# Key and value tiles as unbroken 512 KB runs of the cache

## The chip, the core and the metric

The kernel runs on one core of one Trainium2 chip. The metric is device time in microseconds, from a set of timed runs, and beside it stands the hardware profile of one execution. The core has a matrix engine (PE, with PEld for its weight loads), a vector engine (DVE), a scalar engine (ACT), a general engine (POOL) and a sequencer (SP, SyncE) from which this kernel issues nearly all its DMAs. Sixteen DMA engines carry the transfers from HBM into the on-chip buffer of 128 partitions.

## What is computed

Decoding of one token for four batch entries, through two layers that share all weights: attention against a cache of 4,096 positions, then a gated dense block, and both once more.

```
x: (4, 1, 512)   k_cache, v_cache: (4, 8, 4096, 128)   wq: (512, 4096)   wo: (4096, 512)
w_gate, w_up: (512, 1792)   w_down: (1792, 512)          all bf16

attention(x): q = x @ wq, 32 heads of 128, four query heads to one key head
              p = softmax(q . k / sqrt(128)) over the 4096 positions
              o = sum over positions of p * v;   return o @ wo
dense(x):     (gelu(x @ w_gate) * (x @ w_up)) @ w_down

x = x + attention(layernorm(x));  x = x + dense(layernorm(x))
x = x + attention(layernorm(x));  x = x + dense(layernorm(x))
```

The sum over positions and the softmax do not depend on the order of the positions, as long as a key and its value carry the same number.

## The kernel before

**Tiles.** For one batch entry and one key head, the keys are 4,096 rows of 256 B, 1 MB in one piece in HBM; the values likewise. Position number is 32 times the partition plus a column from 0 to 31: `(p c) d -> p c d`. A tile is one half of the columns (t = 0 or 1, 16 columns, `CH`), so 128 partitions x 4,096 B = 512 KB. In HBM a tile is every other 4 KB of the head's 1 MB.

**Keys.** `Keys` loads the sixteen key tiles of one batch entry, group of four heads by group, and in a group first all t = 0, then all t = 1. `load` (L405) takes one tile with one DMA (L409); `load_pairs` (L411) takes the same half of two neighbouring heads in one DMA of 1 MB (L416). Buffers are `KP`, two heads to a buffer; `KT` are views of one head in it. `turn` transposes a key tile in place on DVE (L424), and `scores` multiplies the turned tile with the queries on PE (L435). The keys of a batch entry stay in the buffer between layer 1 of this entry and its layer 2.

**Values.** `VRing` holds seven slots (`V_SLOTS`) of one tile each. Its list `seq` names the tiles in the order in which they will be needed, and `pump` (L527) issues a DMA (L533) for the next ones as soon as a slot is free. `Values.step` multiplies a tile's sixteen columns with the probabilities on PE (L576), gives the slot back and pumps again. `Streamed.fill` (L611) does it for the values of layer 2 that are taken up while the next dense layer runs (PE at L625). At the end, in `attend_last`, the key buffers are free, and `pump_head` (L536) loads both halves of a value head into one pair buffer with one DMA of 1 MB (L540); some single tiles go into key buffers too, by `pump`.

**Order.** The order of all work is written out by hand. Batch entries run one after another: dense layer of entry b, then `attend(b + 1)`, which does layer 2 of entry b and layer 1 of entry b + 1. The first entry has `attend_first`, the last `attend_last` and `dense_last`. All loads are issued from SP (`dq`) in program order, each behind the wait for its buffer; the weights of the output projection and the dense block (`load_rest`) are loaded once, after the first attention. The lines of the tile's source:

```
def cache_tile(cache, b, kvh, t):
    return cache[b, kvh].rearrange("(p c) d -> p c d", p=P)[:, t * CH:(t + 1) * CH]
...
dq.dma_start(out=KT[kvh][t], in_=cache_tile(A_k_cache, self.b, kvh, t))      # L409
dq.dma_start(out=v, in_=cache_tile(A_v_cache, *key[1:]))                      # L533
```

Of the kernel before, what the change touches and what calls it, by code (L numbers as in the profile page):

```python
# [15 lines left out]
P = 128  # L16
# [9 lines left out]
GH = 4  # L26
CH = 16
# [6 lines left out]
def kernel(  # L34
# [24 lines left out]
    NT = C // CH  # L59
# [25 lines left out]
    dq = nc.sync  # L85
# [6 lines left out]
    KP = [[[wts.tile([P, 2, CH, Dh], BF16, name=f"kp{g}_{t}_{j}") for j in range(GH // 2)]  # L92
           for t in range(NT)] for g in range(NG)]
# [35 lines left out]
        return v.unsqueeze(1).broadcast_to([P, WIDE // n, n])  # L129

    def cache_tile(cache, b, kvh, t):
        return cache[b, kvh].rearrange("(p c) d -> p c d", p=P)[:, t * CH:(t + 1) * CH]

    def load_wq(g):
        n = HG * Dh
# [258 lines left out]
    class Keys:  # L394
# [10 lines left out]
        def load(self, count):  # L405
            for _ in range(count):
                kvh, t = self.tile(self.nl)
                self.nl += 1
                dq.dma_start(out=KT[kvh][t], in_=cache_tile(A_k_cache, self.b, kvh, t))  # L409

        def load_pairs(self, count):  # L411
            for _ in range(count):
                kvh, t = self.tile(self.nl)
                self.nl += 2
                pair = A_k_cache[self.b, kvh:kvh + 2].rearrange("h (p c) d -> p h c d", p=P)
                dq.dma_start(out=KP[kvh // GH][t][kvh % GH // 2][:],  # L416
                             in_=pair[:, :, t * CH:(t + 1) * CH])

        def turn(self, count=1):
            for _ in range(count):  # L420
# [96 lines left out]
    class VRing:  # L517
# [9 lines left out]
        def pump(self, spare=None):  # L527
            free = self.free if spare is None else spare
            while self.at < len(self.seq) and free:
                key = self.seq[self.at]  # L530
                self.at += 1
                v = free.pop(0)
                dq.dma_start(out=v, in_=cache_tile(A_v_cache, *key[1:]))  # L533
                self.ready[key] = (v, spare is None)

        def pump_head(self, pair):  # L536
            (layer, b, kvh, t), other = self.seq[self.at:self.at + 2]
            assert t == 0 and other == (layer, b, kvh, 1)
            self.at += 2
            dq.dma_start(out=pair.rearrange("p t c d -> p (t c) d"),  # L540
                         in_=A_v_cache[b, kvh].rearrange("(p c) d -> p c d", p=P))
            for t in range(NT):
                self.ready[(layer, b, kvh, t)] = (pair[:, t], False)

# [498 lines left out]
```

## Time and profile before

| what | value |
|---|---|
| timed runs, median (lowest to highest of 3) | 306.95 us (304.64 to 307.58) |
| profiled execution, span from first to last instruction | 303.8 us (the page gives no other time of it) |
| mean granted TensorE clock | 0.788 |
| busy: PE, PEld, DVE, ACT, POOL | 193.5, 133.4, 157.0, 43.5, 0.7 us |
| read from HBM over the span | 106.17 MB, 350 GB/s |
| DMA from value cache to v_t | 103 of 512 KB, median 7.9 us from issue to landing |
| DMA from key cache to kp | 40 of 512 KB (13.2 us) and 12 of 1 MB (6.0 us) |
| DMA from value cache to kp | 3 of 1 MB (12.3 us) and 3 of 512 KB (12.0 us) |

An engine's busy time is the time in which it worked on an instruction; weight loads overlap matmuls, and several engines work side by side, so the times are not to be added. The DMA share is the mean busy share of the sixteen DMA engines, and a packet's time in it may overlap the next one's a little, so that a share of 1.02 to 1.03 is a full queue. The time from issue to landing holds the wait behind earlier loads in the queue. A wait names what released it last.

### The profile page before, as it was taken

The page shows a single profiled execution, that of the slowest core. Times are in us where ns is not written, and L with a number is a line of the kernel's source. Part 1 is how long each engine was busy: PE and PEld are TensorE (multiplying, and loading weights), DVE is VectorE, ACT ScalarE, POOL GpSimd, SP SyncE. Part 2 cuts the span into 40 slices and gives each one's busy share as a digit, 9 for nine tenths or more (in the row PEclk, how much of TensorE's full clock was granted, in tenths as well). Part 3 has the DMA queues.
Part 4 walks back from the last instruction along what each step waited for, and adds up shares of the span by engine and source line. Part 5 has one row for each costly group of instructions (what it writes and reads, how often), then busy time and mean ns, then how long its engine had stood idle before and what let it go on. Part 6 is the DMA issues. An engine that isn't in the chain of part 4 may idle for free.

```text
span 303.8 us, 10133 instructions
## 1 busy us (share of the span) xinstructions
PE 193.5 (64%) x4593; PEld 133.4 (44%) x4593; DVE 157.0 (52%) x399; ACT 43.5 (14%) x109; POOL 0.7 (0%) x6
## 2 busy tenths in 40 slices
PE   1466085342684837778838367799373678889884
PEld 0214044332642524556616144566161355565673
DVE  3584913002238896326568983155579931454323
ACT  2001002000012020213201202032121020132200
POOL 0000000000000000000000000000000000000000
PEclk9999997555558675969996859689958597589977
DMA  6999999999439999999999999999999999988900
GB/s 252 367 420 422 416 416 410 368 401 407 173 109 371 404 420 417 417 401 320 344 352 417 419 419 416 412 274 338 357 412 415 420 412 358 337 288 308 415 36 5
DMA packets 32898, 106.83 MB, mean 352 GB/s; under 512 B 2772, under 2 KB 8664, under 8 KB 32472
## 3 DMA queue, kind: packets, MB, share of 16 engines
q1 hardware_dynamic: 32840, 106.19, 90.3%
q8 instruction: 36, 0.59, 0.8%
q14 instruction: 6, 0.05, 0.1%
q10 hardware_dynamic: 16, 0.00, 0.0%
HBM read 106.17 MB, written 0.00 MB: 350 GB/s over the span
## 4 chain that ended last, share of the span: by engine, by line
DMA 61%; PE 25%; DVE 5%; SPq 5%; issue 2%; ACT 1%; DVEq 0%; ACTq 0%
DMA v_t<-in_A_v_cache_dram 34%; DMA kp<-in_A_k_cache_dram 21%; DMA wd_sb<-in_B_w_down_dram 5%; PE sc L435 5%; PE ot L576 4%; PE q L224 4%; PE so L625 3%; PE g L224 2%; SPq L141 2%; PE yr L286 2%; DVE qb L249 1%; PE y L224 1%; DVE pp L462 1%; SPq L142 1%; PE x L481 1%
## 5 line engine op out<-in xcount | busy, mean ns | idle before, releaser
L424 DVE STREAM_TRANSPOSE kp<-kp 128x1024 f32<-128x1024 f32 x64 | 75.4, 1216 | 7.3 <-DMA kp<-in_A_k_cache_dram 7.3
L576 PE MATMUL ot<-pe,v_t 128*128 128x32 bf16 x1520 | 50.2, 184 | 29.6 <-DMA v_t<-in_A_v_cache_dram 26.1
L576 PEld LDWEIGHTS <-v_t 128*128 128x128 bf16 x1520 | 45.3, 102 | 44.4 <-DMA v_t<-in_A_v_cache_dram 33.2
L435 PE MATMUL sc<-kp,qb 128*32 128x512 bf16 x512 | 46.9, 457 | 13.8 <-DVE kp L424 10.2
L435 PEld LDWEIGHTS <-qb 128*32 128x32 bf16 x512 | 14.6, 104 | 34.5 <-issue 18.3
L454 ACT ACTIVATE pp<-sc,nm 128x512 bf16<-128x512 f32 x16 | 11.0, 687 | 128.7 <-DVE junk L450 106.7
L515 DVE TENSOR_TENSOR OT_bf<-ot,rden 128x32 bf16<-128x32 f32 (+3 forms) x34 | 6.0, 176 | 43.9 <-PE ot L576 43.8
L224 PE MATMUL q<-xb,wq_sb 128*128 128x32 bf16 (+1 forms) x640 | 18.5, 176 | 7.0 <-DMA wq_sb<-in_A_wq_dram 7.0
L224 PEld LDWEIGHTS <-wq_sb 128*128 128x128 bf16 x640 | 17.3, 99 | 10.9 <-DMA wq_sb<-in_A_wq_dram 8.0
L441 DVE TENSOR_REDUCE m<-sc 128x1 f32<-128x512 f32 x16 | 10.9, 680 | 15.0 <-PE sc L435 14.9
L481 PE MATMUL x<-pp,ident_bf 128*32 128x128 bf16 x256 | 8.2, 260 | 15.4 <-DVE pp L462 15.4
L467 PE MATMUL den<-zx,mean_f 128*128 128x16 f32 x32 | 8.4, 340 | 13.2 <-DVE qb L249 13.2
L224 PE MATMUL y<-OT_bf,wo_sb 128*128 128x32 bf16 x256 | 8.8, 187 | 8.0 <-DMA wo_sb<-in_A_wo_dram 7.5
L467 PEld LDWEIGHTS den<-zx,mean_f 128*128 128x128 f32 x32 | 6.8, 265 | 15.7 <-issue 15.2
L481 PEld LDWEIGHTS <-ident_bf 128*32 128x32 bf16 x256 | 5.5, 109 | 18.0 <-issue 17.3
L625 PE MATMUL so<-v_t,pl 128*32 128x512 bf16 x96 | 11.5, 470 | 1.0 <-DMA v_t<-in_A_v_cache_dram 0.7
L224 PEld LDWEIGHTS <-wo_sb 128*128 128x128 bf16 x256 | 8.1, 103 | 8.8 <-DMA wo_sb<-in_A_wo_dram 8.0
L224 PE MATMUL g<-xb,wg_sb 128*128 128x32 bf16 x280 | 9.0, 187 | 4.2 <-DMA wg_sb<-in_B_w_gate_dram 3.1
L462 DVE STREAM_TRANSPOSE pp<-pp 128x512 bf16<-128x512 bf16 x16 | 11.1, 691 | 0.9 <-ACT pp L454 0.9
L304 DVE TENSOR_TENSOR xb<-XX,y 128x4 bf16<-128x4 f32 (+1 forms) x9 | 1.6, 173 | 18.2 <-PE y L224 18.2
L224 PEld LDWEIGHTS <-wg_sb 128*128 128x128 bf16 x280 | 8.1, 104 | 5.7 <-DMA wg_sb<-in_B_w_gate_dram 3.2
L224 PE MATMUL u<-xb,wu_sb 128*128 128x32 bf16 x280 | 8.6, 183 | 2.6 <-DMA wu_sb<-in_B_w_up_dram 2.6
(120 smaller groups left out, 169.3 us busy)
## 6 DMA issues: line engine op xcount, KB each, us to landing
v_t<-in_A_v_cache_dram SPq DMA_DIRECT2D x103, 512.0 KB, 7.9
kp<-in_A_k_cache_dram SPq DMA_DIRECT2D x40, 512.0 KB, 13.2
kp<-in_A_k_cache_dram SPq DMA_DIRECT2D x12, 1024.0 KB, 6.0
wq_sb<-in_A_wq_dram SPq DMA_DIRECT2D x2, 2048.0 KB, 11.5
wo_sb<-in_A_wo_dram SPq DMA_DIRECT2D x4, 1024.0 KB, 6.6
kp<-in_A_v_cache_dram SPq DMA_DIRECT2D x3, 1024.0 KB, 12.3
wg_sb<-in_B_w_gate_dram SPq DMA_DIRECT2D x1, 1792.0 KB
wu_sb<-in_B_w_up_dram SPq DMA_DIRECT2D x1, 1792.0 KB
```

The lines of the kernel that those rows point to most:

```text
L141: dq.dma_start(out=wo_sb[:, i * n:(i + 1) * n], in_=wo_dram[:, i * n:(i + 1) * n])
L224: nc.tensor.matmul(dst, lhsT=lhsT, rhs=rhs, start=first, stop=last, skip_group_check=True)
L286: nc.tensor.matmul(self.rows[j:j + B], lhsT=self.o[:, i], rhs=wo_sb[:, i], start=False, stop=True, skip_group_check=True)
L424: nc.vector.transpose(out=words, in_=words)
L435: nc.tensor.matmul(sc[s * QS:(s + 1) * QS], lhsT=qb[:, w0:w0 + 2 * W], rhs=kt[:, :, be // 2, :, be % 2], start=(t == 0 and be == 0), stop= ...
L441: nc.vector.tensor_reduce(out=m[:], in_=sc.rearrange("p c j -> p (c j)"), axis=AX.X, op=ALU.max)
L454: nc.scalar.activation(out=pp[:], in_=sc[:], func=ACT.Exp, bias=nm[:, 0:1], scale=scale, accum_out=ls[:])
L462: nc.vector.transpose(out=flat, in_=flat)
L467: nc.tensor.matmul(den[:], lhsT=mean_f[:, 0:1].broadcast_to([P, P]), rhs=zx[:], start=True, stop=True)
L481: nc.tensor.matmul(x[a * QS:(a + 1) * QS, s], lhsT=ident_bf[:, s * QS:(s + 1) * QS], rhs=pT[:, a], start=True, stop=True, skip_group_check ...
L576: nc.tensor.matmul(self.ot[:, s % 2], lhsT=v[:, i, :], rhs=wide(pe[:, s, t * CH + i, :]), start=(done == 0 and i == 0), stop=(done == NT - ...
L625: nc.tensor.matmul(ps[j * QS:(j + 1) * QS], lhsT=pe[:, s, w:w + 2 * QD].rearrange("p c h -> p (c h)"), rhs=v[:, j * QD:(j + 1) * QD].rearr ...
```

## The change

A position's number becomes 2,048 times t plus 16 times the partition plus a column from 0 to 15, for keys and values alike. Tile t is then the first or the second half of the head's positions, one piece of 512 KB in HBM, of which each partition takes the next 4 KB. Pairs of key heads take such a piece of each of the two heads. `pump_head` still loads the whole 1 MB of a head into the same buffer, but a partition's 8 KB now come from two places 512 KB apart.

```diff
     def cache_tile(cache, b, kvh, t):
-        return cache[b, kvh].rearrange("(p c) d -> p c d", p=P)[:, t * CH:(t + 1) * CH]
+        return cache[b, kvh].rearrange("(t p c) d -> t p c d", t=NT, p=P)[t]
...
-                pair = A_k_cache[self.b, kvh:kvh + 2].rearrange("h (p c) d -> p h c d", p=P)
-                dq.dma_start(out=KP[kvh // GH][t][kvh % GH // 2][:],
-                             in_=pair[:, :, t * CH:(t + 1) * CH])
+                pair = A_k_cache[self.b, kvh:kvh + 2].rearrange("h (t p c) d -> t p h c d",
+                                                                t=NT, p=P)
+                dq.dma_start(out=KP[kvh // GH][t][kvh % GH // 2][:], in_=pair[t])
...
-            dq.dma_start(out=pair.rearrange("p t c d -> p (t c) d"),
-                         in_=A_v_cache[b, kvh].rearrange("(p c) d -> p c d", p=P))
+            dq.dma_start(out=pair[:],
+                         in_=A_v_cache[b, kvh].rearrange("(t p c) d -> p t c d", t=NT, p=P))
```

## The prediction

> **What bounds the kernel now.** I read the DMA row of the page's slices first, then the DMA queues, the chain that ended last, the table by stretches, SP's waits and last the single packet records of the trace.
>
> The DMA rows of the slices (mean busy tenths of the 16 DMA engines, then GB/s, 7.6 us to a slice):
>
> ```profile
> DMA  6999999999439999999999999999999999988900
> GB/s 252 367 420 422 416 416 410 368 401 407 173 109 371 404 420 417 417 401 320 344 352 417 419 419 416 412 274 338 357 412 415 420 412 358 337 288 308 415 36 5
> ```
>
> The DMA engines work nearly all the time, but at two speeds: about 416 GB/s in long stretches, and 270 to 370 GB/s in others where the busy digit is still 9. The only long holes are slices 10 and 11 (nothing left to load before the first dense layer ends) and the last two (all data in).
>
> The queue that carries all loads, with its packets, MB and share of 16 engines over the span, and the heads of the chain:
>
> ```profile
> q1 hardware_dynamic: 32840, 106.19, 90.3%
> ...
> DMA 61%; PE 25%; DVE 5%; SPq 5%; issue 2%; ACT 1%; DVEq 0%; ACTq 0%
> ```
>
> 106.19 MB at 416 GB/s is 255 us of the 303.8 us span. DMA is 61% of the chain, and 34% plus 21% of the span in it are value and key tiles, the very loads that change.
>
> The table by stretches (start and end, length, busy time of PE, PEld, DVE, ACT, POOL, then TensorE's granted clock, DMA share and GB/s):
>
> ```profile
> 8.00:12.00 4.00, 2.14 (x68) 1.97 (x68) 0.81 (x5) 0.00 (x0) 0.00 (x0) 1.00 0.97 328
> 12.00:52.00 40.00, 19.80 (x337) 11.18 (x337) 24.50 (x38) 3.34 (x8) 0.00 (x0) 0.96 1.02 418
> 88.00:104.00 16.00, 11.47 (x277) 8.11 (x270) 12.00 (x25) 3.23 (x8) 0.00 (x0) 0.73 0.97 361
> 104.00:136.00 32.00, 20.68 (x457) 13.37 (x451) 18.45 (x37) 3.93 (x9) 0.00 (x0) 0.76 1.02 415
> 136.00:148.00 12.00, 10.72 (x275) 7.66 (x275) 7.03 (x28) 3.75 (x10) 0.00 (x0) 0.93 0.93 336
> 148.00:161.00 13.00, 6.93 (x173) 4.67 (x165) 8.54 (x20) 2.65 (x7) 0.00 (x0) 0.89 0.96 348
> 197.00:210.00 13.00, 11.79 (x296) 8.44 (x296) 7.56 (x31) 3.75 (x10) 0.00 (x0) 0.92 0.95 324
> 210.00:222.00 12.00, 5.91 (x146) 3.87 (x139) 7.01 (x18) 1.78 (x5) 0.00 (x0) 0.90 0.93 333
> 253.00:275.00 22.00, 18.61 (x459) 13.03 (x459) 8.99 (x35) 4.33 (x11) 0.00 (x0) 0.75 0.89 318
> ```
>
> In the fast stretches the share is 1.02 at 415 to 418 GB/s. In the packet records the median 4,096 B packet there takes 159 ns, and in 12 to 52 us only 8 of 4,066 take over 165 ns. So every engine moves one row after another at its own pace, and the memory's order of addresses does not show. The slow stretches begin where loads start again after a pause or after a change of source: keys at 8, 88, 148 and 210 us, late values beside a dense layer at 136, 197 and 253 us. There the share is 0.89 to 0.97 and the rate a fifth lower, since some 4 KB packets take 250 to 700 ns. Over the whole run, time above the usual for the packet's size (159 ns for 4,096 B, 309 for 8,192, 140 for 3,584, 46 for 1,024) sums to 13.1 us per DMA engine. That is all that a better order of addresses could give back: 4.8 us of it lie in the four key stretches (0.67, 1.48, 1.29, 1.39), 5.7 us in the three beside dense layers (1.24, 2.05, 2.36), the rest is spread.
>
> SP's waits tell why late loads cost time: only seven value slots exist.
>
> ```profile
> SPq L533 <- PE ot L576: 39.9, 44, 4.4
> SPq L533 <- DMA v_t<-in_A_v_cache_dram: 35.4, 41, 4.4
> SPq L409 <- DMA kp<-in_A_k_cache_dram: 29.2, 16, 3.5
> ```
>
> **The change, part by part.** No instruction on PE, DVE, ACT or POOL changes. A position's partition and column are renumbered the same way for keys and values, so softmax weights still meet their own value rows, and sums over positions are the same up to order. Waits, slots and the order of issues on SP stay. Only the source addresses of the cache loads move.
>
> *Single tiles (L409 x40, L533 x106).* Each still moves 128 rows of 4,096 B, one per partition. The step from a row to the next falls from 8 KB to 4 KB. Could the unbroken 512 KB be moved in larger packets? The three 1 MB loads of L540 answer that: their source is already an unbroken 1 MB, and the records show exactly 384 packets of 8,192 B, 128 each, one per partition row. So I count 128 packets of 4,096 B as before, 159 ns each: 0 us. The cost of an issue (328 ns median at L533, 341 at L409) is bounded by the 556 ns of L540. It is beside transfers: a 512 KB tile takes 1.24 us at 420 GB/s, so even 0.23 us more per issue is hidden while several loads are queued. At the seven starts from an empty queue it would show, 7 x 0.23 = 1.6 us at most. I take 0.
>
> *Pairs (L416 x12).* Still 256 packets of 4,096 B, two heads 1 MB apart: 0 us.
>
> *Head loads at the end (L540 x3).* Here the change cuts rows: 128 packets of 8,192 B become 256 of 4,096 B. Each engine has 24 large packets now (384/16); two small ones take 318 ns against 309, so 24 x 9 ns = 0.2 us in all. It is on the path, since the last values land at 290.9 us and nothing but their use and the last dense layer follows: +0.2 us.
>
> *The order of addresses.* This is the one unknown. With an 8 KB step, 16 engines that start together are 32 KB apart (four partition rows each); with a 4 KB step, 16 KB. The trace has no 512 KB unbroken tile, so I bound it from both sides. From below: the extra packet time goes by half everywhere it is on the path, -5.2 us, or wholly, -10.5. From above: it doubles, +10.5 us. The nearest row is again L540: rows without gaps, same engine spacing of 32 KB. From 277 to 280 us its start loses 0.66 us per engine, as much as the start of the keys at 8 us (0.67 us, with gaps). The next nearest, the weight rows at 14 KB engine spacing (66 to 74 us), shows 3,584 B packets at 140 ns almost without exception, but not from an empty queue. I take the row it is nearest to, 0 us.
>
> Here a page bears on it. The Trainium skill, "DMA: Bandwidth & Descriptors", section "Where 436 GB/s comes from", says that for loads from HBM the HBM side binds, at about 358 GB/s; by that a kinder order of addresses might quicken every stretch, by no stated amount. The 415 to 418 GB/s of the fast stretches speak against it here, and the measurement decides.
>
> Sum: 0 + 0 + 0.2 + 0 = +0.2 us on the span of 303.8 us, so 304.0 us. The page shows no other time of the profiled execution; the runs' median, 306.95 us, stands 3.15 us above the span (launch and end, and the spread of the runs, 304.64 to 307.58). I carry the difference over: 307.1 us. About 1% is what a measurement of this kernel can tell from no change.
>
> **The rivals.**
>
> *Faster: starts lose less.* If engines that start together meet in the same parts of memory because their addresses are equal below 32 KB, then half the spacing and rows that fill every 4 KB spread them. For it: the loss sits at starts and fades within 3 us while the queue stays full (8.9 to 11.5 us). Against it: L540's unbroken rows start no better. Price: half of the 4.8 us in the key stretches, where the chain is DMA (10 to 14 us pieces), gives -2.4 us. Half of the 5.7 us beside dense layers adds up to -2.8 us, but there PE is busy 10.7 of 12, 11.8 of 13 and 18.6 of 22 us, and the next wait is PE's. Middle: -4 us, 303 us; if all goes, 296.5. Beside this mechanism stands the Trainium skill's same page, section "Latency and other measured facts", which tells of slower copies at row pitches of 512 KB and more and advises laying tiles out without gaps. Its pitches are far above the 8 KB here, which runs at full pace in this trace.
>
> *Slower: all 16 engines in half the region.* A tile's reads fall in 512 KB instead of 1 MB, with engines 16 KB apart. If that puts more of them on the same part of the memory, the extra time at starts grows, and in the worst case steady packets too. Doubling the starts costs +4.8 us for keys alone, +10.5 with the dense stretches; I take +7, 314 us. Steady packets: 22,784/16 = 1,424 of 4 KB per engine, so each ns more than 159 costs 1.4 us; from 2.2 ns on it is a loss of over 1% by itself. For it: nothing in the trace reads unbroken rows at 16 KB engine spacing. Against it: 1 KB weight rows, whose engines are 4 KB apart, run at 46 ns each in 60 to 64 us with no slow packet, and at 385 GB/s.
>
> *It does not do what it says.* The DMA cuts rows by partition anyway, so a run without gaps is no larger transfer. This is part of my forecast and gives the same 307 us.
>
> **How the numbers follow.** No change within 1%, as forecast: 0.42 (304 to 310 us). Faster by over 1%: 0.31 (296 to 304). Slower by over 1%: 0.27 (310 to 320). I hold the outer two high because the one thing that moves is what the trace cannot show. The range leaves out nearly complete removal of the losses below and more than a doubling above: 299.5 to 315 us.
>
> **What would show it.** Right: packets on the queue rise by 384, the 12 to 52 us stretch stays at 415 to 420 GB/s, and the stretches that start at 88, 148 and 210 us at 330 to 365. Faster: these three rise towards 400 and the key pieces of the chain shrink by 1 to 2 us each, with PE's waits for v_t (26.1 us) falling. Slower: share near 1.0 with fewer GB/s in stretches that now run at 415, or longer key pieces. I would be wrong at the root if packets of another size than 4,096 B appeared for the tiles, or if issues at L533 took much over 328 ns.

## The result, and the profile after

The changed kernel takes 301.42 us (median of 4 runs, 299.87 to 303.08) against 306.9 us for the kernel before, timed beside it (304.64 to 307.58). The ratio is 0.985, with a 95% interval of 0.980 to 0.990. Two later timings gave 0.985 (0.980 to 0.990) and 0.984 (0.977 to 0.991). The forecast was 307.1 us and no change within 1%. The time lies inside the range given with it, 299.5 to 315 us, but the gain is clear of no change. Times here and below are medians of all timed runs, and ratios compare the fast runs alone, so a ratio can differ from the quotient of two medians.

The profiled execution took 300.6 us, and its span is 298.6 us: 2.0 us lie around the span. The prediction had carried over 3.15 us; the rest is taken to be the spread of the runs.

The page of the changed kernel: the DMA rows of the slices, the queue of all loads, and the head of the chain.

```profile
DMA  6999999999619999999999999989999999999900
GB/s 242 419 418 421 420 416 402 338 394 415 239 58 407 417 419 417 418 416 348 327 381 420 416 420 390 402 297 342 358 416 415 420 417 415 379 314 361 376 17 3
...
q1 hardware_dynamic: 33224, 106.19, 91.0%
...
DMA 58%; PE 25%; DVE 7%; SPq 5%; ACT 2%; issue 2%; ACTq 0%; DVEq 0%
```

Packets rose by 384 (32,840 to 33,224), the cut rows of the three head loads, and by nothing else; every tile is still 128 packets of 4,096 B with a median of 159 ns. The second slice has 419 GB/s where it had 367, the thirteenth 407 where it had 371. The fast slices stay at 415 to 421 GB/s.

The table by stretches, with the same columns as in the prediction:

```profile
8.00:12.00 4.00, 2.01 (x68) 1.93 (x68) 0.76 (x4) 0.00 (x0) 0.00 (x0) 1.00 1.03 421
12.00:52.00 40.00, 20.04 (x358) 11.69 (x357) 24.28 (x38) 3.35 (x8) 0.00 (x0) 0.96 1.02 417
88.00:104.00 16.00, 11.91 (x278) 7.97 (x271) 12.95 (x26) 3.23 (x8) 0.00 (x0) 0.74 1.00 397
104.00:136.00 32.00, 22.28 (x490) 14.39 (x490) 17.88 (x40) 4.92 (x12) 0.00 (x0) 0.75 1.02 415
136.00:148.00 12.00, 10.72 (x269) 7.46 (x266) 7.00 (x25) 2.75 (x7) 0.00 (x0) 0.94 0.95 334
148.00:161.00 13.00, 6.41 (x176) 4.85 (x173) 8.08 (x20) 2.64 (x7) 0.00 (x0) 0.88 0.99 388
197.00:210.00 13.00, 11.90 (x291) 7.98 (x291) 7.35 (x28) 3.50 (x9) 0.00 (x0) 0.93 0.92 316
210.00:222.00 12.00, 6.43 (x183) 4.82 (x180) 8.13 (x20) 2.65 (x7) 0.00 (x0) 0.89 1.00 389
253.00:275.00 22.00, 18.87 (x502) 13.63 (x504) 11.14 (x43) 4.83 (x13) 0.00 (x0) 1.00 0.97 352
```

The last two numbers of each row tell the story. In the four stretches where keys start, the rate rose: 328 to 421, 361 to 397, 348 to 388 and 333 to 389 GB/s. In the steady stretches of the table nothing moved (417 against 418, and 415 twice). In the stretches of late values beside a dense layer, 136 to 148 and 197 to 210 us, nothing improved (334 against 336, 316 against 324). The packet records say the same in extra time per DMA engine, counted as in the prediction: 4.83 us in the four key stretches before (0.67, 1.48, 1.29, 1.39), 1.75 after (0.00, 0.54, 0.57, 0.64); 5.65 us in the three late stretches before, 5.78 after.

Two more profiles of the changed kernel bound this. Both have 419 GB/s from 8 to 12 us and 411 and 405 from 88 to 104 us. From 148 and 210 us one has 387 and 385 GB/s, but the other is no faster there than the kernel before (348 and 333):

```profile
148.00:161.00 13.00, 7.14 (x176) 4.77 (x169) 8.46 (x20) 2.64 (x7) 0.00 (x0) 0.89 0.93 353
210.00:222.00 12.00, 6.00 (x142) 3.93 (x135) 7.66 (x18) 2.42 (x7) 0.00 (x0) 0.91 0.91 326
```

So the first two starts improve in every profile, and the third and fourth, which stand behind late value tiles, in two of three.

The landmarks of the two traces, by the end of the maximum over a group's scores (L441), place the first gains. The first group's (24.9 us before) comes 0.44 us earlier. The last group of the second key stretch (96.0 us) comes 1.07 us earlier, of which 1.0 arose within that stretch. The corresponding one at 220.5 us comes 2.6 us earlier. The addition before the last dense layer (L304, 294.8 us before) comes 5.8 us earlier, but 1.7 us of that arise between 259.8 and 270 us of before, where a dense layer runs. Over 253 to 275 us the granted TensorE clock was 0.75 in the profile of before and 1.00 in this one, in a stretch in which PE is busy 85% of the time. In two more profiles of the changed kernel this clock was 0.87 and 0.84, and the same addition came 4.6 and 2.8 us earlier than in that of before. One pair of profiles thus can't be trusted to 1 us; the ratio of the timed runs can.

### The profile page after: what moved, and what is told of

Same layout as the page of the kernel before. It is cut to its first block, busy times and chain, and to the rows that moved or that the text cites. A ratio compares the mean times of both kernels' runs of the same rounds, so it can differ in the third digit from the quotient of the medians.

```text
span 298.6 us, 10129 instructions
## 1 busy us (share of the span) xinstructions
PE 193.4 (65%) x4589; PEld 133.2 (45%) x4593; DVE 156.2 (52%) x399; ACT 43.5 (15%) x109; POOL 0.7 (0%) x6
## 3 DMA queue, kind: packets, MB, share of 16 engines
q1 hardware_dynamic: 33224, 106.19, 91.0%
## 4 chain that ended last, share of the span: by engine, by line
DMA 58%; PE 25%; DVE 7%; SPq 5%; ACT 2%; issue 2%; ACTq 0%; DVEq 0%
DMA v_t<-in_A_v_cache_dram 29%; DMA kp<-in_A_k_cache_dram 24%; PE sc L435 6%; DMA wd_sb<-in_B_w_down_dram 5%; PE q L224 4%; PE ot L576 4%; SPq L141 2%; PE so L625 2%; PE yr L286 2%; PE y L224 1%; PE g L224 1%; DVE pp L462 1%; PE x L481 1%; ACT pp L454 1%; DVE qb L249 1%
## 5 line engine op out<-in xcount | busy, mean ns | idle before, releaser
L576 PE MATMUL ot<-pe,v_t 128*128 128x32 bf16 x1520 | 49.2, 183 | 26.2 <-DMA v_t<-in_A_v_cache_dram 22.6
L576 PEld LDWEIGHTS <-v_t 128*128 128x128 bf16 x1520 | 44.7, 101 | 41.3 <-DMA v_t<-in_A_v_cache_dram 27.9
L435 PE MATMUL sc<-kp,qb 128*32 128x512 bf16 x512 | 48.8, 485 | 12.6 <-DVE kp L424 9.1
L441 DVE TENSOR_REDUCE m<-sc 128x1 f32<-128x512 f32 x16 | 10.9, 680 | 16.5 <-PE sc L435 16.4
L467 PE MATMUL den<-zx,mean_f 128*128 128x16 f32 x32 | 8.6, 347 | 11.3 <-DVE qb L249 11.3
L304 DVE TENSOR_TENSOR xb<-XX,y 128x4 bf16<-128x4 f32 (+1 forms) x9 | 1.6, 173 | 18.6 <-PE y L224 18.6
L625 PE MATMUL so<-v_t,pl 128*32 128x512 bf16 x96 | 10.6, 434 | 0.9 <-DMA v_t<-in_A_v_cache_dram 0.9
```

The source lines that it names most:

```text
L435: nc.tensor.matmul(sc[s * QS:(s + 1) * QS], lhsT=qb[:, w0:w0 + 2 * W], rhs=kt[:, :, be // 2, :, be % 2], start=(t == 0 and be == 0), stop= ...
L441: nc.vector.tensor_reduce(out=m[:], in_=sc.rearrange("p c j -> p (c j)"), axis=AX.X, op=ALU.max)
L467: nc.tensor.matmul(den[:], lhsT=mean_f[:, 0:1].broadcast_to([P, P]), rhs=zx[:], start=True, stop=True)
L576: nc.tensor.matmul(self.ot[:, s % 2], lhsT=v[:, i, :], rhs=wide(pe[:, s, t * CH + i, :]), start=(done == 0 and i == 0), stop=(done == NT - ...
L625: nc.tensor.matmul(ps[j * QS:(j + 1) * QS], lhsT=pe[:, s, w:w + 2 * QD].rearrange("p c h -> p (c h)"), rhs=v[:, j * QD:(j + 1) * QD].rearr ...
```

## The experiments

Two theories to begin with. **S**: the starts of the key loads lose less. **V**: the gain comes from value tiles or from the head loads at the end. After the first answers the question became why the starts lose: **G**, gaps between a tile's rows; **A**, engines 32 KB or a multiple of it apart; **B**, all rows of a tile in 4 KB blocks of one parity, since a step of 8, 16 or 24 KB never leaves the parity and one of 4, 12 or 20 KB changes it with every row.

**Keys alone.** From the kernel before; value tiles and head loads stay, so keys and values no longer match, and the result is not the reference's. The same holds for most kernels below; the bytes moved are equal in all.

```diff
-                dq.dma_start(out=KT[kvh][t], in_=cache_tile(A_k_cache, self.b, kvh, t))
+                dq.dma_start(out=KT[kvh][t], in_=run_tile(A_k_cache, self.b, kvh, t))
...
-                in_=pair[:, :, t * CH:(t + 1) * CH]
+                in_=pair[t]        # pair: "h (t p c) d -> t p h c d"
```

> Key tiles unbroken, value tiles and head loads as before, so keys and values no longer carry the same position number: the result is not the reference's, the work and the bytes are the same. Theory S (starts of the key loads lose less when a tile is unbroken): almost the whole gain, -3 to -5 us against before; the stretch from 8 to 12 us runs at 420 GB/s instead of 328, and the stretches from 88, 148 and 210 us at 385 to 400 instead of 333 to 361. Theory V (the gain comes from value tiles or the last head loads): within 1 us of before, key stretches at 330 to 360 GB/s.

It took 303.5 us, ratio 0.996 (0.992 to 1.000). The stretches:

```profile
8.00:12.00 4.00, 2.15 (x68) 1.97 (x68) 0.89 (x5) 0.00 (x0) 0.00 (x0) 1.00 1.03 423
88.00:104.00 16.00, 11.26 (x274) 7.77 (x271) 13.12 (x26) 3.23 (x8) 0.00 (x0) 0.88 1.00 404
148.00:161.00 13.00, 6.58 (x181) 4.97 (x178) 8.00 (x20) 2.64 (x7) 0.00 (x0) 0.84 1.01 377
210.00:222.00 12.00, 6.00 (x152) 3.70 (x144) 6.28 (x16) 1.09 (x3) 0.00 (x0) 0.99 0.96 345
```

The first two starts are as fast as in the changed kernel. The third and fourth, whose keys queue behind late value tiles, are in between. S is right about the place and wrong that it is all.

**Values and head loads alone.**

> Value tiles and head loads changed, keys as before (again positions of keys and values do not match: not the reference's result). Theory S: within 1.5 us of before, key stretches as slow as before (8 to 12 us at 328 GB/s), and the stretches beside dense layers unchanged, since their loss is that of a thin queue. Theory V: -4 to -5 us, with the stretches of late values above 340 GB/s.

It took 305.36 us, ratio 1.003 (1.000 to 1.007), with 337 GB/s from 8 to 12 us and 365 from 88 to 104, as before. That spoke for S, until it was repeated. From 148 and 210 us it had 360 and 345 GB/s, a little above before.

**All but the head loads.** L540 keeps its form from before.

> All of the change but the three 1 MB head loads, which keep one 8 KB row per partition (their positions then do not match the keys': not the reference's result). The prediction counted the cut rows at +0.2 us: then this is 0.2 us faster than the changed kernel, which no timing shows, but the records would show 309 ns packets. Rival: the cut rows start better (extra packet time after 275 us fell from 0.96 to 0.23 us per engine), then this is 0.5 to 1 us slower than the changed kernel.

It took 300.64 us, ratio 0.989 (0.983 to 0.996), beside 299.76 us for the whole change (next). The intervals overlap; neither 0.2 us of cost nor a gain of the cut rows can be told. The packet records tell more. From 2 to 14 us after the first head issue, the extra time per engine is 0.71 us before and 0.65 us here, with 8 KB rows, and 0.64, 0.62 and 0.59 us in three profiles of the whole change, with 4 KB rows from two halves. In these five profiles the loss at the start of the head loads stays whatever their form (in the other kernels it is 0.45 to 0.55 us with 8 KB rows and 0.31 to 1.15 with 4 KB rows, so the size scatters); that less of it lies after 275 us in the changed kernel only means that the loads come earlier.

**The change once more.**

> The changed kernel once more, beside the others on one chip: 299 to 303 us, ratio 0.98 to 0.99 to before. Where its gain comes in is read against before by the same stretches.

299.76 us, ratio 0.985 (0.980 to 0.990); 419 GB/s from 8 to 12 us and 411 from 88 to 104.

**The step between rows.** Four kernels in which single and pair tiles of both caches take rows of 4 KB at a step of 12, 16, 20 or 24 KB; the head loads are the change's. For 12 KB:

```diff
+    def spread(cache, b, kvh, t, n=1):
+        at = min((b * Hkv + kvh) * Sk, (B * Hkv - n + 1) * Sk - P * 48) + t * CH
+        src = cache[0, 0]
+        dims = [[48 * Dh, P]] + ([[Sk * Dh, n]] if n > 1 else []) + [[Dh, CH], [1, Dh]]
+        return bass.AP(tensor=src.tensor, offset=src.offset + at * Dh, ap=dims)
...
-                dq.dma_start(out=v, in_=cache_tile(A_v_cache, *key[1:]))
+                dq.dma_start(out=v, in_=spread(A_v_cache, *key[1:]))
```

> All of the change, but single and pair tiles of keys and values take 4 KB rows at a step of 12 KB (other rows of the cache than the reference's; the same bytes and packets). Engines that start together are 48 KB apart. Theory G (gaps between rows cost, 8 KB of 12 are left out): as slow as before or slower, 305 us or more, 8 to 12 us at 330 GB/s or less. Theory A (starts lose where engines are 32 KB or a multiple of it apart, at equal addresses below 32 KB): as fast as the changed kernel, 299 to 302 us, 8 to 12 us at 415 GB/s or more.

> The same with a step of 16 KB, engines 64 KB apart. Theory G: slower than with 12 KB, 306 us or more. Theory A: starts as bad as before or worse, 305 to 310 us, 8 to 12 us at 330 GB/s or less.

> The same with a step of 20 KB, engines 80 KB apart. Theory G: slower than with 16 KB, 308 us or more. Theory A: as fast as the changed kernel, 299 to 302 us.

> The same with a step of 24 KB, engines 96 KB apart, three times 32 KB. Theory G: the slowest of the four. Theory A: as before, 305 us or more, 8 to 12 us at 330 GB/s.

First the 12 KB step, its stretches from 8 and 88 us:

```profile
8.00:12.00 4.00, 2.14 (x68) 1.97 (x68) 0.85 (x5) 0.00 (x0) 0.00 (x0) 1.00 1.02 417
88.00:104.00 16.00, 11.52 (x271) 8.14 (x271) 13.55 (x27) 3.23 (x8) 0.00 (x0) 0.76 1.01 407
```

The 16 KB step:

```profile
8.00:12.00 4.00, 2.15 (x68) 1.97 (x68) 0.84 (x5) 0.00 (x0) 0.00 (x0) 1.00 1.00 354
88.00:104.00 16.00, 11.09 (x288) 7.96 (x282) 11.08 (x25) 3.23 (x8) 0.00 (x0) 0.86 0.92 353
```

The 20 KB step:

```profile
8.00:12.00 4.00, 2.14 (x68) 1.97 (x68) 0.81 (x5) 0.00 (x0) 0.00 (x0) 1.00 1.03 423
88.00:104.00 16.00, 11.27 (x271) 7.81 (x272) 13.71 (x27) 3.23 (x8) 0.00 (x0) 0.89 1.01 408
```

The 24 KB step:

```profile
8.00:12.00 4.00, 2.15 (x68) 1.97 (x68) 0.81 (x5) 0.00 (x0) 0.00 (x0) 1.00 1.01 394
88.00:104.00 16.00, 11.98 (x281) 8.18 (x274) 12.05 (x26) 3.23 (x8) 0.00 (x0) 0.73 0.96 362
```

Read the last number of each row down the steps. With the two kernels already known it goes fast, slow, fast, slow, fast, slow:

| step (engine spacing, KB) | GB/s 8 to 12 us | GB/s 88 to 104 us | extra us per engine, 8 to 12 | the same, 2 to 16 us after the first pair's issue (86 to 88 us) | ratio to before |
|---|---|---|---|---|---|
| 4 KB (16), the change | 421 | 397 | 0.00 | 0.19 | 0.985 (0.980 to 0.990) |
| 8 KB (32), before | 328 | 361 | 0.67 | 1.07 | 1 |
| 12 KB (48) | 417 | 407 | 0.00 | 0.17 | 0.977 (0.968 to 0.986) |
| 16 KB (64) | 354 | 353 | 0.54 | 0.51 | 0.996 (0.991 to 1.002) |
| 20 KB (80) | 423 | 408 | 0.00 | 0.11 | 0.983 (0.975 to 0.990) |
| 24 KB (96) | 394 | 362 | 0.19 | 0.85 | 0.998 (0.993 to 1.003) |

G falls. A tile with two thirds or four fifths of the region left out starts as well as an unbroken one. The odd steps give the whole gain and the even ones none (the ratios at 12 and 20 KB rest on four executions each, so their order among the odd steps means nothing); that a tile is unbroken is not what helps. The spacing in the table rests on the prediction's count of four rows to an engine, which no record here shows.

The even steps are not alike, and A did not get their size: for 16 and 24 KB it expected 330 GB/s or less from 8 to 12 us, and 354 and 394 came. Why 24 KB loses so little there (0.19 us), and still 0.85 us behind the pairs, is open.

The column for the pairs leaves out the first 2 us after their issue, since these belong to another loss. The pairs start from an empty queue, and in those 2 us 0.41 us per engine is lost before, 0.32, 0.36 and 0.30 in three profiles of the change, 0.40 and 0.72 at 12 and 20 KB, 0.44 and 0.35 at 16 and 24 KB: no order by step. What the odd step takes away comes behind that, when the queue has filled.

Beside these rows a page can be read again: the Trainium skill, "DMA: Bandwidth & Descriptors", section "Latency and other measured facts", tells that for copies between HBM tensors at a row pitch of 4 MB a pad of 4 KB restored the full rate and one of 192 B did not, and infers, as not verified, that the partitions' streams, in lock-step, meet in the same HBM channels. The runs here agree that an odd 4 KB in the step makes the difference, and show it already at a step of 8 KB, where only starts lose; whether channels are behind it, no run here shows.

**Spacing or parity.** A single step of rows can't separate A from B: if the engines start four rows apart, as the prediction counts, an even number of 4 KB in the step is always a multiple of 32 KB in the spacing. The next two kernels take two pieces of 2 KB, 4 KB apart, from each step, and the second head of a pair 4 KB further on. A tile then has blocks of both parities. From the 12 KB kernel:

```diff
-        dims = [[48 * Dh, P]] + ([[Sk * Dh, n]] if n > 1 else []) + [[Dh, CH], [1, Dh]]
...
+        if n > 1:
...
+            dims = [[step * Dh, P], [(Sk + CH) * Dh, n], [1, CH * Dh]]
+        else:
...
+            dims = [[step * Dh, P], [CH * Dh, 2], [1, CH // 2 * Dh]]
```

> Single tiles of keys and values take from each step of 8 KB two pieces of 2 KB, 4 KB apart, and a pair's second head is taken 4 KB further on: engines stay 32 KB apart, but a tile no longer reads only one of each two 4 KB blocks (other rows of the cache than the reference's). Twice the packets for single tiles: from 46 ns for 1 KB and 159 ns for 4 KB a 2 KB packet is estimated at 84 ns, so both kernels of this pair are some 8 us slower than with whole rows. Theory A (engine spacing of 32 KB): the stretch from 8 to 12 us is slow, extra packet time of 0.4 us per engine or more, and this kernel is 3 to 6 us slower than its twin with a step of 12 KB. Theory B (all rows of a tile in blocks of one parity of 4 KB): no loss at 8 to 12 us, under 0.15 us, and no difference from the twin beyond 1.5 us.

> The twin: the same two pieces of 2 KB, 4 KB apart, and the same shift of a pair's second head, but a step of 12 KB, engines 48 KB apart. Both theories: no loss from 8 to 12 us (under 0.15 us per engine), 305 to 310 us for the greater number of packets.

They took 312.66 us (ratio 1.022, 1.013 to 1.031) and 307.49 us (1.005, 1.000 to 1.009). The step of 8 KB:

```profile
8.00:12.00 4.00, 2.14 (x68) 1.97 (x68) 0.89 (x5) 0.00 (x0) 0.00 (x0) 1.00 1.04 404
88.00:104.00 16.00, 10.96 (x272) 7.94 (x268) 10.82 (x24) 3.23 (x8) 0.00 (x0) 0.81 0.96 336
```

The step of 12 KB:

```profile
8.00:12.00 4.00, 2.14 (x68) 1.97 (x68) 0.81 (x5) 0.00 (x0) 0.00 (x0) 1.00 1.05 406
88.00:104.00 16.00, 11.61 (x282) 7.78 (x275) 12.37 (x26) 3.23 (x8) 0.00 (x0) 0.81 0.97 377
```

Neither theory holds alone. For the single tiles that start at 8 us, mixed parity took the loss away at a spacing of 32 KB (0.00 us of extra time; 404 GB/s is full pace for 2 KB packets, whose median is 84 ns): B. For the pairs that start at 88 us it did not (336 GB/s, 2.09 us per engine from 80 to 104 us, against 0.59 for the twin), and the times differ by 5.2 us as A had it. All of these 2.09 us lie in the 4 KB packets of the pairs; the 2 KB packets of the single tiles that follow lose nothing there either.

Were the short pieces the cure at 8 us, rather than the mix? The same two pieces of 2 KB, but 8 KB apart at a step of 16 KB, so that all lie in blocks of one parity (pairs take whole rows at a step of 16 KB):

```diff
-            dims = [[step * Dh, P], [CH * Dh, 2], [1, CH // 2 * Dh]]        # step = 32
+            dims = [[step * Dh, P], [2 * CH * Dh, 2], [1, CH // 2 * Dh]]    # step = 64
```

> Single tiles take from each step of 16 KB two pieces of 2 KB, 8 KB apart, so all pieces lie in 4 KB blocks of one parity (other rows of the cache than the reference's; pairs take whole 4 KB rows at a step of 16 KB). If the parity matters: the stretch from 8 to 12 us loses 0.3 us per engine or more. If the short pieces took the loss away: under 0.1 us there.

```profile
8.00:12.00 4.00, 2.03 (x68) 1.95 (x68) 0.76 (x4) 0.00 (x0) 0.00 (x0) 1.00 1.08 338
```

The loss is back (338 GB/s, 0.86 us per engine, from a single execution, which took 314.04 us). It does not end there: from 12 to 52 us this kernel runs at 391 GB/s with 1.31 us of extra time, where the 8 KB step with mixed parity has 407 GB/s and 0.15 us. The spacing by the prediction's count is 64 KB here and was 32 KB there, both of which lose with whole rows. So for single tiles the evidence is for the parity. For pairs, one reading is that all engines read first one head and then the other, so that at any moment they still share a parity; that is argued, no run shows it.

**Do layouts have to match?** Keys unbroken, single value tiles at a step of 12 KB.

> Keys unbroken as in the changed kernel, single value tiles with 4 KB rows at a step of 12 KB (other rows of the value cache than the reference's). Theory A: both spacings are odd multiples of 16 KB, so as fast as the changed kernel, 298 to 302 us, and the first experiment was slow for its value tiles' spacing. Theory M (keys and values laid out differently cost when they share the queue): as the first experiment, 303 us or more, stretches from 148 and 210 us at 345 to 380 GB/s.

302.99 us, ratio 0.988 (0.976 to 1.001). The time lies on the border between the two expectations, but the stretches behind late values ran at 392 and 402 GB/s, where keys alone had 377 and 345 (384 in a second profile, next). That is as fast as the change at its best (388 and 389), so two layouts in one queue are no cost to see there.

**Do the parts add up?** Keys alone again, on another chip:

> The first experiment once more (keys unbroken, values as before). If parts do not add up, again 302 to 305 us with the first two key stretches fast (8 to 12 us at 420 GB/s, 88 to 104 at 400) and those from 148 and 210 us between before and changed; if its first result was chance, 299 to 302 us.

303.18 us, ratio 0.990 (0.979 to 1.001); 424, 408, 377 and 384 GB/s in the four key stretches. Then three kernels side by side: keys alone, single value tiles alone, the whole change.

> Keys unbroken, values and head loads as before. If the parts add up: 1.2 to 1.6% faster than before, the same as the changed kernel beside it within 1 us. If keys and values must change together: 0.3 to 0.9%, 1.5 us or more slower than the changed kernel beside it.

> Only the single value tiles unbroken; keys and head loads as before (positions of keys and values do not match: not the reference's result). If the parts add up: within 0.4% of before. If value tiles carry a part of their own: 0.5% faster or more.

> The changed kernel beside the two: 1.3 to 1.7% faster than before.

They took 303.78 us (ratio 0.994, 0.989 to 0.999), 303.5 us (0.991, 0.987 to 0.995) and 300.25 us (0.984, 0.977 to 0.991). The value tiles alone leave the first starts slow:

```profile
8.00:12.00 4.00, 2.04 (x68) 1.96 (x68) 0.76 (x4) 0.00 (x0) 0.00 (x0) 1.00 0.96 331
88.00:104.00 16.00, 11.41 (x276) 8.16 (x272) 11.61 (x25) 3.23 (x8) 0.00 (x0) 0.71 0.95 356
148.00:161.00 13.00, 6.94 (x163) 4.46 (x156) 8.48 (x20) 2.64 (x7) 0.00 (x0) 0.91 0.99 377
210.00:222.00 12.00, 5.69 (x145) 3.60 (x136) 6.88 (x18) 1.65 (x4) 0.00 (x0) 0.92 0.98 361
```

but raise the third and fourth (377 and 361 GB/s against 348 and 333 before), where value tiles still stand ahead of the keys in the queue. This contradicts the first result for values, so both forms were timed again side by side.

> Value tiles and head loads changed, keys as before, a second time. If the cut rows of the head loads cost: again within 0.4% of before and 1.5 us or more slower than the twin beside it. If the first result was chance: 0.5 to 1% faster than before, within 1 us of the twin.

> Only the single value tiles changed, a second time: 0.5 to 1.3% faster than before if the first result holds, within 0.4% if it was chance.

304.84 us (ratio 0.990, 0.985 to 0.995) and 303.65 us (0.988, 0.980 to 0.996). The first result for values did not repeat; its interval (1.000 to 1.007) does not meet these, and what differed then is not known. The head loads show no cost that repeats. So keys alone gave 0.4, 1.0 and 0.6%, values alone 0.9 to 1.2% in three of four timings, both together 1.5 to 1.6%. The parts add up as far as these intervals reach.

## Why the prediction was wrong

**The bound** was read rightly: DMA, at full pace in steady stretches, with losses where loads start. The steady stretches did not move, and the total that could be won, 13.1 us of extra packet time per engine, fell to 10.3 (11.3 and 10.4 in two more profiles of the change).

**The size of the packets and the issues** came as counted: 128 packets of 4,096 B to a tile, 384 more packets in all, 0 us for tiles and pairs. The +0.2 us for the cut head rows lie below what the timings resolve.

**The step that failed** is "The order of addresses": of the ends -10.5 and +10.5 us it took "the row it is nearest to, 0 us", from the start of the three head loads. That row has a loss of the same size but of another kind. It stands behind a nearly drained queue, like the late values, and e3 and the changed kernel show that such a start loses 0.6 to 0.7 us in either form. The keys at 8 us start behind a full queue (share 0.97, and 0.67 us lost), though the prediction counts them among "seven starts from an empty queue"; there the step between rows decides all of it: 0.00 us at every odd step. From 88 us both losses stand in a row, the first 2 us at every step and then 1.07 us that falls to 0.19. The prediction had both rows, equal to 0.01 us, and read one as evidence on the other. Of the rows at another spacing that ran behind a full queue, it set the weights at 14 KB (3 slow packets in 1,024) aside for not starting from an empty queue, and used the 1 KB weight rows against the slower rival only; they were the better neighbours.

**The rival that came true** is "starts lose less", at 0.31 and 303 us. Its mechanism, addresses equal below 32 KB, fits the order of the six steps, but not the single tiles of mixed parity, which start at a spacing of 32 KB without loss; what is shown is the odd step. Its terms: half of the 4.8 us in key stretches was asked for, 3.1 us went in the first profile, 2.6 and 1.9 in two others of the same kernel (second stretch counted from 80 us, since the pairs come earlier there). Half of the 5.7 us beside dense layers, up to 2.8 us, was asked for and nothing came: 5.4 to 7.1 us are lost there at every step of whole rows that was tried. The argument against this rival, "L540's unbroken rows start no better", was the mix-up above.

**What stays open.** Extra packet time in key stretches fell by 1.9 to 3.1 us per engine, and the time by 1.5%, about 4.6 us. The signs that the prediction had named came in the main. Rates in key stretches rose towards 400, but for the third and fourth start in one profile of three. PE's waits for v_t fell from 26.1 to 22.6, 23.2 and 21.1 us. The chain's key pieces in the first changed profile begin at other issues (12.45, 13.58 and 13.45 us for 11.38, 12.96 and 14.28) and can't be compared. In the two others they begin at the same issue, the second single key tile of each batch entry. Before, and in the second profile of the change:

```profile
93.12 11.38 DMA kp<-in_A_k_cache_dram
153.37 12.96 DMA kp<-in_A_k_cache_dram
215.24 14.28 DMA kp<-in_A_k_cache_dram
...
92.16 10.11 DMA kp<-in_A_k_cache_dram
151.05 12.62 DMA kp<-in_A_k_cache_dram
213.24 13.39 DMA kp<-in_A_k_cache_dram
```

The third profile has 10.00, 12.22 and 13.18 us. Each piece is thus 0.3 to 1.4 us shorter, and with the first entry's two pieces (24.94 us before, 24.07 and 23.96 after) the sum falls by 3.4 and 4.2 us. That comes near the 4.6 us, but not run by run: these two spans are 4.8 and 2.9 us shorter than that of before.

Not every change of source to an even step loses, either. In the kernel before, the second half of wq (4 KB rows at a step of 8 KB) and the keys behind it follow at about 19 and 24 us, placed by the bytes of the issues, with the queue full. From 17 to 30 us 0.00 us per engine is lost. What sets the start at 8 us apart from these two, no run here shows.

**The slower rival** (engines in half the region) found no support: at 16 KB of spacing the starts lose less than at 32 KB, and steady packets keep their 159 ns.

## What to carry to other kernels

When many DMA engines start together on rows at a fixed step, look at the step in units of 4 KB: steps of 1, 3 and 5 units ran from the first microseconds at 417 to 423 GB/s here, steps of 2, 4 and 6 began at 328 to 394. What helps is the odd step; an unbroken tile is merely the easiest way to get one. In steady flow neither mattered with whole 4 KB rows (416 to 418 GB/s from 12 to 52 us at all six steps). These are rows of 4 KB in one kernel on one core; the only other rows tried, two pieces of 2 KB, also lost in steady flow when all lay in one parity (391 GB/s). When an unknown is bounded by the nearest row, make sure that its loss is of the same kind: the start of the head loads behind a drained queue and that of the keys behind a full one lost the same 0.7 us here, and only the second could be won.

## What was not expected of the hardware

Starts lose in two ways, about alike in size. A step of 8 KB costs 0.67 us in the first 4 us of the keys, with the queue full all the while, and next to nothing in the 40 us of steady flow that follow (0.13 us of extra time per engine from 12 to 52 us, in the kernel before). A start from an empty queue cost 0.3 to 0.7 us at any step: so it was in the first 2 us of the pairs at 86 to 88 us, at all six steps of whole rows. And three profiles of the changed kernel have spans of 298.6, 299.0 and 300.9 us, beside granted TensorE clocks of 1.00, 0.87 and 0.84 over 253 to 275 us.
